# Attention with memories and a relu² MLP in one program: instructions left in the order of the kernel's own list schedule

## The chip, the cores and the metric

The kernel runs on one core of a Trainium2 chip. The metric is the device time of one execution in microseconds (us). A core has a matrix engine (PE in the profile), a vector engine (DVE), a scalar engine (ACT), a general engine (POOL), and a queue that starts transfers (SP). Each engine runs its own instructions one after the other and waits on semaphores for the others.

## The reference

Eight batches of eight heads, 576 tokens, head width 64, 32 memories. Attention reads from memories that are themselves sums over the tokens, and a two-layer MLP follows.

```python
a = softmax(phi, axis=2)                      # (8, 8, 576, 32), over the tokens' 32 weights
k_m = einsum('bhsm,bhsd->bhmd', a, k)         # 32 memories per head
v_m = einsum('bhsm,bhsd->bhmd', a, v)
attn = softmax(q @ k_m^T / 8) @ v_m           # (8, 8, 576, 64)
x = attn.transpose(0, 2, 1, 3).reshape(4608, 512)
out = relu(x @ w_in) ** 2 @ w_out             # w_in 512 x 2048, w_out 2048 x 512, given as 64-bit floats
```

## The kernel before

**What is computed in which form.** Products are wanted to the accuracy of 32-bit floats, so that each operand of the large products is split in a high and a low part (fp32r), and three products are summed: high by high, high by low, low by high. The kernel does not form x. For each batch it keeps the attention weights (ath high, atl low: 256 rows, as 8 heads of 32 memories, by 576 tokens), and for each slice of 256 of the 2048 hidden columns the product of the memories' values with w_in, called vw. The hidden product is then h = vw by at (L740), with a contraction of 256 instead of 512.

**Weights.** They come as 64-bit floats and are read as pairs of 32-bit words into a tile "raw" (L322). `decode` (L310 to L364) makes a high and a low part of them with some five DVE instructions (L324 to L357), ACT casts and, for some blocks, three PE matmuls into a tile pd. The parts of w_in are also written back to memory (L364, by POOL's queue), from which `wi_again` (L369, by SP's queue) reloads them for later pairs of batches. w_out's parts stay on the chip as 16 tiles wo. All decoding lies in the first 200 us or so.

**Order of the work.** Batches 0 and 1 go first, mixed with the decoding (n=0). Then come pairs of batches n=1, 2, 3 (batches 2 and 3, 4 and 5, 6 and 7). For a pair: `memory` makes the memories of its heads from phi, k and v; `attention` the weights at; then, for each slice s of 8, `vw_step` (L525 to L547) makes vw for both batches of the pair in two halves hh=0, 1, and two `step`s of the first batch use it. A step g is one block of 128 hidden columns of one batch (128 steps in all; batch 4 has steps 64 to 79). The second batch's 16 steps follow with the same vw.

**A vw half.** Six matmuls (L536) sum into one PSUM tile pvw (tag pv, one bank for all of them). Then, for each half of 64 partitions and each of two column ranges, ACT casts a piece of the tile into the high part of vw (L260, 64 by 256) and DVE subtracts that from the tile to get the low part (L545): four casts and four subtractions before the bank is free for the next pvw.

**A step.** `mm1` multiplies the two token ranges (0 to 256 is h_0, 256 to 576 is h_1; two PSUM banks for h), with six matmuls each (L740). A relu into r follows on ACT (L744) or DVE (L745), whichever the planner chose; then on ACT the square gh of the first 512 tokens, rounded to fp32r (L746), and gl of the last 64 (L747); the exact square r² of all 576 (L748 on ACT, or L749 on DVE); and on DVE the low parts glo (L750) and gl (L751). `mm2` adds to four accumulators acc: for each a matmul with gh and wo's high part (L770) and one with its low part (L771), then one with glo (L773). `mm2_left` (L796) does the last 64 tokens of both batches. At a batch's end the accumulators are copied and stored.

**What sets the order.** None of the functions issues anything at once. Each records operations with `plan.op`: the engines that may do it with an assumed duration, what it reads and writes, and a closure. `Plan.order` (L99 to about L184) is a list schedule: from assumed durations and latencies it works out a due time for each operation, then hands each engine, at each moment, the ready operation that is due first. In this schedule an operation can start once those before it in its data and its buffers have ended, and casts and subtractions of one pvw tile may overlap. The result is sorted by planned start time, and the last loop (L905) calls the closures in this order, which emits the instructions. The framework under it (`tile.TileContext`) tracks tiles, sets the semaphores, and has a scheduler of its own, which in the kernel before may still place the emitted instructions of each engine in another order.

Of the kernel before, what the change touches and what calls it, by code (L numbers as in the profile page):

```python
# [206 lines left out]
def tile_attention_moe(  # L207
# [41 lines left out]
    plan = Plan()  # L249
# [652 lines left out]
        for ff in range(NFF):  # L902
            step(pos[b1, ff])

    for o in plan.order():  # L905
        o.fn(o.left)


# [28 lines left out]
```

## Time and profile before

| what | value |
|---|---|
| median of 3 runs (their range) | 814.89 us (814.53 to 815.09) |
| the profiled execution, and its span | 814.6 us, all of it span |
| instructions | 13267 |
| PE busy | 776.2 us, 95% |
| DVE, ACT, POOL busy | 66%, 49%, 8% |
| read and written in memory | 79.17 MB, 17.83 MB |

A row of the timeline gives the start, the duration, the engine, the line, the operation, the tile written and those read with their shapes, how many instructions the row joins (x2), and in brackets the idle time of the engine before it with what ended it. Matmuls are pipelined, so that a row's duration is longer than the step from one matmul to the next. A row that joins instructions may enclose others that begin between its own. PEld is the loading of weights into PE, which goes on beside its matmuls.

### The profile page before, as it was taken

How to read it: one execution, taken by the hardware profiler on the slowest of the kernel's cores; microseconds unless marked ns; L12 is line 12 of the kernel's file. 1: busy time of each engine (PE TensorE's matmuls, PEld its weight loads, DVE VectorE, ACT ScalarE, POOL GpSimd, SP SyncE). 2: the span in 40 equal slices, each digit the busy share in tenths (PEclk: the TensorE clock that was granted, in tenths of full speed). 3: DMA queues.
4: the chain of work that ended last, by engine and by line, in shares of the span. 5: the costliest groups of instructions: out<-in, count | busy, mean ns of one | idle time of the engine just before them, and what ended most of it. 6: DMA issues, size and time to landing. Idle time of an engine off the chain costs nothing.

```text
span 814.6 us, 13267 instructions
## 1 busy us (share of the span) xinstructions
PE 776.2 (95%) x4926; PEld 652.5 (80%) x4926; DVE 536.4 (66%) x1190; ACT 403.1 (49%) x922; POOL 63.8 (8%) x103
## 2 busy tenths in 40 slices
PE   4889999999999999999999999999999999999995
PEld 2567888778887888888778888888788888888884
DVE  4678888783468976766776556877677556864540
ACT  2557766675653465634445355644334355643220
POOL 4012202320100100010000100010000100000000
PEclk9999999999999999999999999999999999999998
DMA  7969967666456523423443433513422433100001
GB/s 225 270 191 286 270 176 239 188 170 191 125 146 189 165 81 105 129 37 90 132 125 88 126 106 104 136 34 91 133 58 70 122 108 104 30 24 29 1 1 64
DMA packets 99716, 101.04 MB, mean 124 GB/s; under 512 B 32260, under 2 KB 85508, under 8 KB 99652
## 3 DMA queue, kind: packets, MB, share of 16 engines
q1 hardware_dynamic: 89188, 81.55, 34.2%
q0 software_dynamic: 10464, 18.65, 8.8%
q8 instruction: 39, 0.64, 0.3%
q14 instruction: 25, 0.20, 0.1%
HBM read 79.17 MB, written 17.83 MB: 119 GB/s over the span
## 4 chain that ended last, share of the span: by engine, by line
PE 73%; DVE 8%; issue 6%; DMA 5%; ACT 4%; SPq 1%; POOL 1%; DVEq 0%; POOLq 0%; ACTq 0%
PE h L740 20%; PE acc L770 12%; PE acc L773 12%; PE acc L771 12%; PE accl L796 5%; PE pvw L536 4%; PE psc L574 3%; PE pkv L426 2%; DMA raw<-in_moe_w_out_dram 1%; DMA phi<-in_phi_dram 1%; ACT vw L260 1%; DMA raw<-in_moe_w_in_dram 1%; DMA wo<-work 1%; DVE glo L750 1%; DVE work L327 1%
## 5 line engine op out<-in xcount | busy, mean ns | idle before, releaser
L740 PE MATMUL h<-ath,vw 128*128 128x320 f32 (+1 forms) x1024 | 211.6, 298 | 1.1 <-ACT r L744 0.6
L770 PE MATMUL acc<-wo,gh 128*128 128x512 f32 x512 | 207.0, 404 | 1.8 <-ACT gh L746 1.6
L771 PE MATMUL acc<-wo,gh 128*128 128x512 f32 x512 | 201.7, 394 | 0.0
L740 PEld LDWEIGHTS h<-ath,vw 128*128 128x128 f32 x1024 | 171.0, 189 | 17.2 <-ACT r L744 1.7
L773 PE MATMUL acc<-wo,glo 128*128 128x512 f32 x512 | 162.1, 405 | 1.7 <-DVE glo L750 1.5
L260 ACT CAST vw<-pvw 64x256 fp32r<-64x256 f32 (+1 forms) x224 | 85.7, 397 | 74.5 <-PE pvw L536 35.4
L545 DVE TENSOR_TENSOR vw<-pvw,vw 64x256 fp32r<-64x256 f32 x192 | 78.8, 420 | 64.8 <-ACT vw L260 62.9
L770 PEld LDWEIGHTS acc<-wo,gh 128*128 128x128 f32 x512 | 96.4, 188 | 23.4 <-ACT gh L746 3.7
L740 PE MATMUL h<-atl,vw 128*128 128x320 f32 (+1 forms) x512 | 109.9, 295 | 0.0
L771 PEld LDWEIGHTS acc<-wo,gh 128*128 128x128 f32 x512 | 96.4, 188 | 16.6
L773 PEld LDWEIGHTS acc<-wo,glo 128*128 128x128 f32 x512 | 89.5, 189 | 19.5 <-DVE glo L750 6.2
L746 ACT ACTIVATE gh<-r 128x512 fp32r<-128x512 f32 x128 | 80.8, 632 | 43.4 <-DVE r L745 37.6
L750 DVE TENSOR_TENSOR glo<-r,gh 128x512 fp32r<-128x512 f32 x128 | 87.5, 684 | 21.4 <-ACT r L748 19.7
L744 ACT ACTIVATE r<-h 128x256 f32<-128x256 f32 (+1 forms) x149 | 60.1, 406 | 56.8 <-PE h L740 53.5
L745 DVE TENSOR_SCALAR r<-h 128x320 f32<-128x320 f32 (+1 forms) x107 | 48.9, 459 | 58.4 <-PE h L740 57.9
L740 PEld LDWEIGHTS h<-atl,vw 128*128 128x128 f32 x512 | 82.5, 189 | 0.7 <-issue 0.2
L747 ACT ACTIVATE gl<-r 128x64 fp32r<-128x64 f32 x128 | 32.8, 256 | 68.5 <-DVE r L745 66.5
L748 ACT ACTIVATE r<-r 128x576 f32<-128x576 f32 x94 | 64.5, 686 | 2.2
L796 PE MATMUL accl<-wo,gl 128*128 128x512 f32 x192 | 52.3, 397 | 0.1
L796 PEld LDWEIGHTS accl<-wo,gl 128*128 128x128 f32 x192 | 35.0, 188 | 7.2 <-DVE o L260 0.5
L536 PE MATMUL pvw<-wi,VTh 128*128 128x256 f32 x192 | 37.3, 286 | 0.6 <-issue 0.3
L749 DVE TENSOR_TENSOR r<-r 128x576 f32<-128x576 f32 x34 | 25.7, 756 | 15.8 <-ACT gh L746 14.4
(137 smaller groups left out, 854.3 us busy)
## 6 DMA issues: line engine op xcount, KB each, us to landing
wi<-w_in_hi SPq DMA_DIRECT2D x56, 256.0 KB
wi<-w_in_lo SPq DMA_DIRECT2D x56, 256.0 KB
KV<-in_k_dram SPq DMA_DIRECT2D x32, 256.0 KB
KV<-in_v_dram SPq DMA_DIRECT2D x32, 256.0 KB
raw<-in_moe_w_in_dram SPq DMA_DIRECT2D x16, 512.0 KB
raw<-in_moe_w_out_dram SPq DMA_DIRECT2D x16, 512.0 KB
q<-in_q_dram SPq DMA_DIRECT2D x24, 288.0 KB
out_dram<-o POOLq DMA_DIRECT2D x20, 256.0 KB, 7.7
```

The lines of the kernel that those rows point to most:

```text
L260: nc.scalar.copy(o, i) if e == "ACT" else ENG[e].tensor_copy(o, i)
L536: nc.tensor.matmul(pw()[:, x * SL:(x + 1) * SL], l()[:, 2 * hh + x, :], w(r, x), start=(i == 0), stop=(i == 2))
L545: vec({"DVE": tt(SL)}, lambda e, V=V, pr=pr, src=src: nc.vector.tensor_sub(V()[pr, 1, hh, :], src(), V()[pr, 0, hh, :].bitcast(F32)), [pw, ...
L740: nc.tensor.matmul(p()[:, 0:n], V()[:, l, hh, c0:c0 + P], x()[:, hh, cs], start=(i == 0), stop=(i == 5))
L744: op({"ACT": act(n) - 30, **({} if b < 2 else {"DVE": tt(n)})}, lambda e, cs=cs, n=n, p=p: nc.scalar.activation(r()[:, cs], p()[:, 0:n], A ...
L746: op({"ACT": act(SM)}, lambda e: nc.scalar.activation(gh(), r()[:, 0:SM], AF.Square), [r], [gh])
L748: op({"ACT": act(S), **({} if b < 2 else {"DVE": tt(S)})}, lambda e: nc.scalar.activation(r(), r(), AF.Square) if e == "ACT" else nc.vecto ...
L750: vec({"DVE": tt(SM)}, lambda e: nc.vector.tensor_sub(glo(), r()[:, 0:SM], gh().bitcast(F32)), [r, gh], [glo])
L770: nc.tensor.matmul(a(), gh()[:, c], t()[:, 0], start=f0, stop=False)
L771: nc.tensor.matmul(a(), gh()[:, c], t()[:, 1], start=False, stop=False)
L773: nc.tensor.matmul(a(), glo()[:, c], t()[:, 0], start=False, stop=f1)
L796: nc.tensor.matmul(a(), G()[:, l, :], t()[:, w], start=(ff == 0 and n == 0), stop=(ff == NFF - 1 and n == 2))
```

## The change

The last loop stands in a `with tc.manual_schedule()`. Inside it the framework places each engine's instructions as they are emitted, that is in the order of `plan.order()`. The operations, the engine of each, the tiles, the buffers and the dependencies between instructions stay as they are; semaphores still make an instruction wait for what it needs.

```diff
-    for o in plan.order():
-        o.fn(o.left)
+    with tc.manual_schedule():
+        for o in plan.order():
+            o.fn(o.left)
```

Three places follow, on three engines; numbers in names are those of batch or step, slice and half, and a running number at the end, which is higher by two after the change.

PE in the first batch of pair n=2, step 68 and slice 3: h68_0 is the first token range of the step, pvw2_3_1 the second half of slice 3. First before, then after.

```order
L740 MATMUL h68_1_5253<-ath4_4838,vw2_0_2_5113 128x320 x2
L740 MATMUL h68_0_5270<-ath4_4838,vw2_0_2_5113 128x256 x2
L740 MATMUL h68_0_5270<-atl4_4852,vw2_0_2_5113 128x256 x2
L740 MATMUL h68_0_5270<-ath4_4838,vw2_0_2_5113 128x256 x2
L536 MATMUL pvw2_3_1_5261<-wi2_3_1_5115,VTh21_4228 128x256 x2
L536 MATMUL pvw2_3_1_5261<-wi2_3_1_5115,VTl21_4233 128x256
L536 MATMUL pvw2_3_1_5261<-wi2_3_1_5115,VTh21_4228 128x256 x2
L536 MATMUL pvw2_3_1_5261<-wi2_3_1_5115,VTl21_4233 128x256
L773 MATMUL acc4_0_2_5061<-wo11_686,glo67_5220 128x512
```

The same place of PE after the change.

```order
L740 MATMUL h68_1_5255<-ath4_4840,vw2_0_2_5115 128x320 x2
L536 MATMUL pvw2_3_1_5263<-wi2_3_1_5117,VTh21_4230 128x256 x2
L536 MATMUL pvw2_3_1_5263<-wi2_3_1_5117,VTl21_4235 128x256
L536 MATMUL pvw2_3_1_5263<-wi2_3_1_5117,VTh21_4230 128x256 x2
L536 MATMUL pvw2_3_1_5263<-wi2_3_1_5117,VTl21_4235 128x256
L740 MATMUL h68_0_5272<-ath4_4840,vw2_0_2_5115 128x256 x2
L740 MATMUL h68_0_5272<-atl4_4854,vw2_0_2_5115 128x256 x2
L740 MATMUL h68_0_5272<-ath4_4840,vw2_0_2_5115 128x256 x2
L773 MATMUL acc4_0_2_5063<-wo11_688,glo67_5222 128x512
```

The pvw product and h68_0 have changed places. The same exchange stands in slices 3 to 6 of n=2 and of n=3, at eight places. In slice 2 of both, two matmuls of a pvw that stood ahead of L773 stand behind it.

ACT at the same step, before: the relu, gl and gh of step 68 and the casts from pvw2_3_1 into the two batches' vw.

```order
L744 ACTIVATE r68_5268<-h68_0_5270 128x256
L747 ACTIVATE gl68_5309<-r68_5268 128x64
L746 ACTIVATE gh68_5297<-r68_5268 128x512
L260 CAST vw2_0_3_5235<-pvw2_3_1_5261 64x256 x2
L748 ACTIVATE r68_5268<-r68_5268 128x576
L260 CAST vw2_1_3_5241<-pvw2_3_1_5261 64x256
L747 ACTIVATE gl69_5325<-r69_5307 128x64
L260 CAST vw2_1_3_5241<-pvw2_3_1_5261 64x256
L746 ACTIVATE gh69_5319<-r69_5307 128x512
```

ACT at the same step, after.

```order
L260 CAST vw2_0_3_5237<-pvw2_3_1_5263 64x256 x2
L260 CAST vw2_1_3_5243<-pvw2_3_1_5263 64x256
L744 ACTIVATE r68_5270<-h68_0_5272 128x256
L260 CAST vw2_1_3_5243<-pvw2_3_1_5263 64x256
L746 ACTIVATE gh68_5299<-r68_5270 128x512
L747 ACTIVATE gl68_5311<-r68_5270 128x64
L748 ACTIVATE r68_5270<-r68_5270 128x576
L746 ACTIVATE gh69_5321<-r69_5309 128x512
```

Three casts have moved ahead of the relu and the fourth ahead of gh68, and gl68 behind gh68. In n=1 the same kind of move puts gl and a cast ahead of r².

DVE near the start, before: the last mx of batch 1's memories, the first glo, and the decoding (work_524) of the block of w_in in raw_410.

```order
L409 TENSOR_REDUCE mx1_1_511<-phi1_1_322 128x128
L750 TENSOR_TENSOR glo0_583<-r0_521,gh0_550 128x512
L751 TENSOR_TENSOR gl0_553<-r0_521,gl0_553 128x64
L451 TENSOR_SCALAR rs1_0_593<-pkv1_0_526 128x1
L452 RECIPROCAL rs1_0_593<-rs1_0_593 128x1
L459 SCALAR_TENSOR_TENSOR kvx1_0_610<-pkv1_0_526,rs1_0_593,par_76 128x128 x2
L324 TENSOR_SCALAR work_524<-raw_410 128x512
L326 TENSOR_SCALAR work_524<-raw_410 128x512
```

DVE at the same place, after.

```order
L409 TENSOR_REDUCE mx1_1_513<-phi1_1_324 128x128
L324 TENSOR_SCALAR work_526<-raw_412 128x512
L326 TENSOR_SCALAR work_526<-raw_412 128x512
L327 SCALAR_TENSOR_TENSOR work_526<-work_526 128x512
L328 TENSOR_SCALAR work_526<-work_526 128x512
L340 SCALAR_TENSOR_TENSOR wi0_1_1_582<-raw_412,work_526 128x512
L750 TENSOR_TENSOR glo0_585<-r0_523,gh0_552 128x512
L751 TENSOR_TENSOR gl0_555<-r0_523,gl0_555 128x64
```

The decoding of the block has moved ahead of glo0 and of batch 1's memory. In the first 200 us some half of DVE's and ACT's instructions stand at other places among their neighbours, on PE about a tenth in the whole program, nearly all of them before 93 us. On SP loads of raw weights and reloads of w_in change places up to the start of n=1, and after it one load of k in each of batches 3 to 7.

## The prediction

> **What bounds the kernel now.** I read the page first, for the engine that carries the span.
>
> ```profile
> span 814.6 us, 13267 instructions
> PE 776.2 (95%) x4926; PEld 652.5 (80%) x4926; DVE 536.4 (66%) x1190; ACT 403.1 (49%) x922; POOL 63.8 (8%) x103
> ```
>
> PE (TensorE) is busy for 776.2 of 814.6 us, no other engine for more than 66%. A change of order removes no work, so it can only move the 38 us in which PE idles. The second view, busy time by stretch, says where those are (columns: stretch, length, busy us and instructions of each engine, granted clock, DMA share, GB/s).
>
> ```profile
> core 0: us, PE busy (x) PEld busy (x) DVE busy (x) ACT busy (x) POOL busy (x), PEclk, DMA share, GB/s
> 0.00:100.00 100.00, 81.51 (x702) 60.00 (x703) 70.61 (x159) 57.34 (x120) 23.58 (x39) 0.98 0.85 246
> 100.00:200.00 100.00, 93.26 (x550) 81.00 (x549) 74.72 (x152) 67.26 (x144) 19.24 (x25) 1.00 0.69 198
> 450.00:520.00 70.00, 69.75 (x391) 60.38 (x390) 42.11 (x96) 34.99 (x89) 3.11 (x5) 1.00 0.39 112
> 640.00:710.00 70.00, 69.75 (x393) 60.42 (x392) 43.61 (x100) 37.38 (x94) 1.33 (x2) 1.00 0.29 87
> ```
>
> PE lacks 18.49 us in the first 100 us and 6.74 in the second 100: 25.23 us, the ceiling of what a better order can win there. In the stages 450 to 520 and 640 to 710 it lacks 0.25 us of 70. There nothing can be won and every new wait is paid in full. These two are the stages in which the next pairs of batches (n=2, n=3) turn their weights into vw, and the order of instructions shows PE, ACT (ScalarE) and DVE (VectorE) changed exactly there. The third view is therefore the timeline of one such period, engine by engine.
>
> **The change, part A: the first wait, for the pvw bank.** All pvw products share one PSUM bank (tag pv), which four ACT casts (L260) and four DVE subtractions (L545) empty. Before, PE does the second half of the hidden product (h68_0, L740) and then the second pvw of the slice; the change puts pvw first. PE around such a place:
>
> ```profile
> 484.37 0.28 PE L536 MATMUL pvw<-wi,VTl 128*128 128x256 f32 x1
> 486.92 0.69 PE L740 MATMUL h<-ath,vw 128*128 128x320 f32 x4
> 487.45 0.40 PE L740 MATMUL h<-atl,vw 128*128 128x256 f32 x2
> 487.93 0.47 PE L536 MATMUL pvw<-wi,VTh 128*128 128x256 f32 x2
> ```
>
> ACT and DVE in the same time (in brackets the idle time before, and what ended it):
>
> ```profile
> 484.68 0.64 ACT L260 CAST vw<-pvw 64x256 fp32r<-64x256 f32 x2 [1.60 <-PE pvw L536]
> 485.80 0.37 ACT L260 CAST vw<-pvw 64x256 fp32r<-64x256 f32 x1 [0.48 <-DVE vw L545]
> 486.65 0.37 ACT L260 CAST vw<-pvw 64x256 fp32r<-64x256 f32 x1 [0.48 <-DVE vw L545]
> ```
> ```profile
> 485.35 0.42 DVE L545 TENSOR_TENSOR vw<-pvw,vw 64x256 fp32r<-64x256 f32 x1 [1.42 <-ACT vw L260]
> 486.20 0.42 DVE L545 TENSOR_TENSOR vw<-pvw,vw 64x256 fp32r<-64x256 f32 x1 [0.43 <-ACT vw L260]
> 487.05 0.77 DVE L545 TENSOR_TENSOR vw<-pvw,vw 64x256 fp32r<-64x256 f32 x2 [0.43 <-ACT vw L260]
> ```
>
> The two engines never read the bank at the same time: cast, cast, subtraction, cast, subtraction, cast, two subtractions, each waiting for the one before. From pvw's end (484.65) to the last subtraction (487.82) this takes 3.17 us. The planner lets casts and subtractions overlap and so expects the bank earlier. PE reaches the new place of pvw when h68_1's last pair of matmuls is issued, one pair's 0.24 us before 487.45: at 487.21. It then stands until the bank is free. Taking 487.93 for that, as now, the wait is 0.72 us.
>
> [...]
>
> **Part A: the second wait, for gh68.** The second change at these places is on ACT: before, relu (L744), gl, gh (L746) and only then the casts of the second pvw; after, the casts are laid around the relu, and gh stands behind the fourth. A period now:
>
> ```profile
> 476.95 0.40 PE L740 MATMUL h<-atl,vw 128*128 128x256 f32 x2
> 477.43 0.47 PE L536 MATMUL pvw<-wi,VTh 128*128 128x256 f32 x2
> 478.10 0.28 PE L536 MATMUL pvw<-wi,VTl 128*128 128x256 f32 x1
> 480.28 0.40 PE L770 MATMUL acc<-wo,gh 128*128 128x512 f32 x1
> 481.89 0.39 PE L771 MATMUL acc<-wo,gh 128*128 128x512 f32 x1
> 482.28 1.20 PE L773 MATMUL acc<-wo,glo 128*128 128x512 f32 x4
> ```
> ```profile
> 477.62 0.39 ACT L744 ACTIVATE r<-h 128x256 f32<-128x256 f32 x1 [1.09 <-PE h L740]
> 478.05 0.62 ACT L746 ACTIVATE gh<-r 128x512 fp32r<-128x512 f32 x1
> 479.33 0.69 ACT L748 ACTIVATE r<-r 128x576 f32<-128x576 f32 x1
> 481.33 0.37 ACT L260 CAST vw<-pvw 64x256 fp32r<-64x256 f32 x1 [0.77 <-DVE vw L545]
> ```
> ```profile
> 481.55 0.67 DVE L750 TENSOR_TENSOR glo<-r,gh 128x512 fp32r<-128x512 f32 x1
> ```
>
> One such period is 10.50 us (pvw at 477.43 and again at 487.93). Let S be the start of the second pvw in the new order. It ends at S+0.95 (477.43 to 478.38). By the durations above: casts one and two to S+1.65, subtraction to S+2.08, cast three to S+2.48, relu to S+2.84 beside two subtractions that end at S+3.37, cast four to S+3.77, gh68 (0.62) to S+4.42. PE itself, with the same matmuls as now between 476.71 (0.24 before 476.95) and 480.28, reaches the first product with gh68 (L770) at S+3.57. Starting at about S+4.45 it waits 0.88 us. Back from this goes 0.15: before L773 PE now stands from 482.13 (481.89 and one step of 0.24) to 482.28 for glo, and in the new order r² and glo are done at S+6.07, while PE has its eight products only at S+6.30.
>
> Together 0.72 + 0.88 - 0.15 = 1.45 us a period. The exchange stands in slices 3 to 6 of n=2 and of n=3, 8 places: **+11.6 us**. Bounds: only the first wait bites and the 0.15 goes, 8 x 0.57 = 4.6; at the other end both, with nothing given back, 8 x 1.60 = 12.8. I take 11.6, since the rows fix each step of the chain; a shift of a few tenths moves one wait into the other rather than away.
>
> **Part B: slice 2 of both stages.**
>
> ```profile
> 471.39 0.42 PE L536 MATMUL pvw<-wi,VTh 128*128 128x256 f32 x2
> 472.02 1.20 PE L773 MATMUL acc<-wo,glo 128*128 128x512 f32 x4 [0.20 <-DVE glo L750]
> ```
>
> Before, two matmuls of a pvw fill PE's wait for glo; after, they stand behind L773. What filled the gap becomes idle: 0.42 us by its row, and up to 0.63, the whole stretch from 471.39 to 472.02. I take 0.54, between the two, twice: **+1.1 us** (0 to 1.3).
>
> **Part C: n=1, about 280 to 340 us.** After, ACT does gl and a third cast before r² (L748).
>
> ```profile
> 299.63 0.69 ACT L748 ACTIVATE r<-r 128x576 f32<-128x576 f32 x1
> 300.38 0.67 DVE L750 TENSOR_TENSOR glo<-r,gh 128x512 fp32r<-128x512 f32 x1
> 302.29 1.09 PE L773 MATMUL acc<-wo,glo 128*128 128x512 f32 x4
> ```
>
> With gl (0.26) and the cast (0.37, behind a subtraction) in front, r² ends at 301.15 instead of 300.32; on DVE two subtractions and a relu then go ahead of glo, which is ready at 302.43, against PE's 302.29. That is 0.15 us in six periods: **+0.9 us** (0 to 2).
>
> **Part D: the first 200 us.** Here the weights are decoded on DVE, and half of all its instructions move.
>
> ```profile
> 47.55 1.27 DVE L409 TENSOR_REDUCE mx<-phi 128x128 f32<-128x640 f32 x1
> 51.75 0.69 DVE L750 TENSOR_TENSOR glo<-r,gh 128x512 fp32r<-128x512 f32 x1 [2.93 <-ACT r L748]
> 53.59 0.41 DVE L324 TENSOR_SCALAR work<-raw 128x512 f32<-128x512 f32 x1
> ```
> ```profile
> 41.08 0.49 SPq L322 DMA_DIRECT2D raw<-in_moe_w_in_dram  x1
> ```
>
> DVE stands 2.93 us for r of the first step, with a block of weights that was asked for at 41.08 lying undecoded until 53.59. After, that block's five DVE instructions stand ahead of glo and can fill the hole. Against that, DVE now waits in order: an instruction whose block is late holds all behind it, glo among them. And PE's need here is set by loads as well (the DMA share is 0.85). The gain has the hole, 2.93 us, and as much again from the other stretch of idle PE as its edge (-5, rounded in); the loss is one such hole put in front of glo (+3). No row fixes the value; I take half a hole, **-1.5 us**.
>
> On SP, decode blocks and reloads of weights change places up to the start of n=1, and after that one load of K in each of batches 3 to 7 moves four places back; on POOL the write-outs of decoded weights change places among themselves. In n=2 and n=3 no load of weights for pvw moves, so I cost the queues at nothing there: the DMA share of 0.29 to 0.39 is the cover. A load that came late all the same would show as a wait before L536. What the queues do in the first 200 us lies within part D's bounds.
>
> Sum: 11.6 + 1.1 + 0.9 - 1.5 = +12.1 us on the profiled execution's 814.6, which lies 0.3 us under the median of the runs, 814.89. Forecast: 814.89 + 12.1 = **827.0 us**.
>
> **The rivals.**
> - *Faster.* The list order was meant for these engines, and the other order hides its loss where PE idles. For it: 25.23 us of idle PE, and the 2.93 us hole. Against it: the two stages with 0.25 us of slack. It needs the waits of part A to vanish, by casts that come earlier than I walk them, B with them, and part D at its edge of -5, with C's 0.9: 814.9 - 5 + 0.9 = 810.8. Chance 0.10.
> - *Half the price.* The periods re-phase, so that only one of the two waits bites: 4.6 + 1.1 + 0.9 - 3 = +3.6, about 818.5. Chance 0.12.
> - *The bank is shared by halves.* Casts and subtractions of different halves overlap: four casts back to back (0.64 a pair, 1.3) and a last subtraction (0.42), 1.7 to 2.1 us, less than the 2.56 from 484.65 to 487.21. Then both waits of part A vanish and B's lasts: 1.1 + 0.9 - 1.5, 815.4. [...] The waits for one another in the rows speak against it, and the change adds no freedom there. Chance 0.04.
> - *No effect,* because the engines' orders come out alike: the order of the changed program excludes it, PE, ACT and DVE differ at the places named. Left is that gains and losses cancel. Chance 0.03.
> - *Slower than forecast.* In-order waits for loads in the first 200 us cost more than a hole: 12.8 + 1.3 + 2 + 3 and a second hole of 3 make +22, so 837. Chance 0.10.
>
> **How the numbers follow.** The forecast itself has 0.61: 827, with 820 to 833 from its terms' bounds. The range goes from 815 (which takes in half price and the shared bank) to 834; outside lie the faster rival and most of the slowest one. A measurement of this kernel can tell some 0.2%, 1.6 us, from no change, so "same" is 813.3 to 816.5. Faster 0.11; same 0.07 (shared bank, cancellation); slower 0.82.
>
> **What would show it.** In the changed trace's stages n=2 and n=3 the period must grow from 10.50 to about 11.95 us; PE idle of 0.7 us before L536, released by DVE vw L545, and of 0.9 before L770, released by ACT gh L746, 8 times each. The idle of PE by stretch should be 6 us higher in each of the two stages, and within a few us of 25 in the first 200. Periods of 10.50 would prove part A wrong; a total change made before 200 us would prove part D wrong, whatever the sum.

## The result and the profile after

The changed kernel takes 827.82 us (median; 827.10 to 829.45) against 814.99 us of the kernel before (four runs, 814.53 to 821.47). The ratio on record is 1.0126, with a 95% interval of 1.0076 to 1.0175; the two medians alone give 1.0157. The forecast was 827.0 in a range of 815 to 834. The profiled executions differ by 11.6 us in span.

The page of the changed kernel, span and busy time:

```profile
span 826.2 us, 13317 instructions
PE 779.5 (94%) x4926; PEld 654.9 (79%) x4926; DVE 538.9 (65%) x1190; ACT 395.6 (48%) x922; POOL 64.5 (8%) x103
```

The count of work instructions is the same on every engine. PE's busy time differs by 3.3 us, so at least the other 8.3 of the 11.6 us are PE standing still. Busy time by stretch says where (columns as in the prediction):

```profile
0.00:100.00 100.00, 82.69 (x710) 63.09 (x711) 72.72 (x162) 58.71 (x123) 24.30 (x39) 0.95 0.84 245
100.00:200.00 100.00, 97.60 (x581) 86.20 (x580) 73.19 (x150) 69.66 (x151) 19.16 (x24) 1.00 0.68 199
280.00:340.00 60.00, 58.96 (x334) 51.05 (x333) 41.11 (x93) 33.04 (x86) 0.00 (x0) 1.00 0.33 99
450.00:520.00 70.00, 63.95 (x348) 54.09 (x347) 37.47 (x86) 31.71 (x81) 2.70 (x4) 1.00 0.34 99
640.00:710.00 70.00, 64.33 (x352) 54.74 (x351) 36.57 (x85) 30.90 (x79) 2.69 (x4) 1.00 0.32 95
```

Two things happened, with opposite signs. In the two stages of n=2 and n=3, PE's idle time rose from 0.25 us to 6.05 and 5.67 in 70 us. Between 100 and 200 us it fell from 6.74 to 2.40 us.

The waits of PE over the whole changed program (total, times, longest) name the two waits that part A of the prediction walked:

```profile
PE acc L770 <- ACT gh L746: 9.0, 13, 1.4
PE pvw L536 <- PE h L740: 4.4, 8, 0.6
```

Eight waits before pvw, and thirteen before the first product with gh: eight at the places of part A, three ahead of these (two in n=2, one in n=3), two in the first 200 us. One place of n=2 in PE's timeline, both waits of it (480.23 to 481.31 belongs to the period before):

```profile
480.23 0.40 PE L740 MATMUL h<-ath,vw 128*128 128x256 f32 x2
481.31 0.50 PE L770 MATMUL acc<-wo,gh 128*128 128x512 f32 x1 [0.68 <-ACT gh L746]
487.76 0.46 PE L740 MATMUL h<-ath,vw 128*128 128x320 f32 x2
488.76 0.48 PE L536 MATMUL pvw<-wi,VTh 128*128 128x256 f32 x2 [0.55 <-PE h L740]
```

and DVE's and ACT's rows that release them:

```profile
487.89 0.77 DVE L545 TENSOR_TENSOR vw<-pvw,vw 64x256 fp32r<-64x256 f32 x2 [0.43 <-ACT vw L260]
```
```profile
491.25 0.38 ACT L744 ACTIVATE r<-h 128x256 f32<-128x256 f32 x1
492.27 0.37 ACT L260 CAST vw<-pvw 64x256 fp32r<-64x256 f32 x1 [0.64 <-DVE vw L545]
492.67 0.63 ACT L746 ACTIVATE gh<-r 128x512 fp32r<-128x512 f32 x1
```

The pair of matmuls at 487.76 hands over after 0.29 us, at 488.05; pvw starts at 488.76, 0.71 us later (forecast 0.72). The row's own figure is 0.55, because the modelled end of the last matmul covers the beginning of a wait. It names PE's h as the releaser, which had long been done: what ended just before is the last subtraction, at 488.66. In the same way PE could go on at 480.47 and starts L770 at 481.31, 0.84 us later (forecast 0.88). And the ACT rows show why: the relu is done at 491.63, and gh, which needs it, starts at 492.67, behind the fourth cast, which itself waits for a subtraction.

The period has grown as forecast. The second pvw of slices 3, 4 and 5 of n=2 in the changed kernel:

```profile
476.74 0.96 PE pvw L536 x6
488.76 0.96 PE pvw L536 x6
500.80 0.96 PE pvw L536 x6
```

That is 12.02 and 12.04 us from one to the next, against 10.50 before (477.43 to 487.93) and 11.95 in the forecast.

**The lead, step by step.** A single time mixes the two signs, so from here on the kernels are compared step by step. Each step g has four L771 matmuls; the start of the first in one trace less that in the trace of before is the kernel's lag at that step (negative: a lead). Step 68 of before, for example, starts its first L771 at 480.51; the changed kernel at 481.65.

| kernel | step 1 | 19 | 31 | 43 | 63 | 66 | 74 | 95 | 98 | 106 | 127 |
|---|---|---|---|---|---|---|---|---|---|---|---|
| the change | 2.96 | -10.28 | -6.25 | -2.45 | -2.27 | -0.17 | 5.63 | 5.07 | 5.78 | 11.81 | 11.52 |
| first200 | 0.35 | -12.88 | -9.06 | -8.52 | -9.12 | -9.12 | -9.12 | -9.03 | -9.06 | -9.08 | -9.03 |
| rest200 | 1.68 | -1.27 | -0.70 | 3.24 | 3.07 | 5.19 | 11.03 | 10.63 | 11.30 | 17.30 | 17.02 |
| gh_first | 6.33 | -6.98 | -3.65 | 0.69 | 0.94 | 3.05 | 6.70 | 7.38 | 8.11 | 11.94 | 12.57 |
| h0_first | 3.61 | -9.66 | -6.08 | -1.57 | -1.34 | 0.79 | 6.58 | 5.99 | 6.65 | 12.59 | 12.38 |
| both_back | 3.79 | -9.48 | -5.90 | -1.44 | -1.69 | 0.42 | 1.01 | 0.85 | 1.58 | 2.24 | 2.20 |
| r2_first | 0.14 | -13.11 | -9.08 | -2.63 | -1.97 | 0.18 | 6.02 | 5.76 | 6.47 | 12.43 | 12.21 |
| glo_first | 3.98 | -9.28 | -4.74 | -1.85 | -1.94 | 0.20 | 6.04 | 5.54 | 6.24 | 12.22 | 12.01 |
| lat | 7.19 | -6.08 | -2.41 | 3.56 | 3.33 | 4.34 | 7.82 | 6.96 | 6.49 | 10.17 | 10.04 |
| first200_dve | 11.19 | -1.23 | 1.95 | 1.87 | 1.74 | 1.74 | 1.77 | 1.17 | 1.11 | 1.07 | 1.09 |
| first200_notdve | 7.17 | -5.99 | -1.23 | -1.38 | -0.88 | -0.88 | -0.87 | -1.35 | -1.41 | -1.41 | -1.36 |
| first150 | 1.95 | -9.13 | -8.80 | -8.91 | -9.28 | -9.28 | -9.30 | -9.52 | -9.58 | -9.61 | -9.60 |

In the kernel before, steps 1, 19 and 31 begin at 58, 189 and 255 us. Steps 0 to 31 are n=0 with the decoding, 32 to 63 n=1, 64 to 95 n=2, 96 to 127 n=3. The eight places of part A lie between steps 66 and 74 and between 98 and 106. The change loses 5.80 and 6.03 us there: 11.83, or 1.48 a place. Two things limit the table. All lags are taken against one trace of before. And equal steps are not quite equal work: ahead of step 1 PE has issued 395 matmuls in the kernel before and 412 in the list's order, while at step 31 both have issued 1679, so that the lag at step 31 compares like with like, and the one at step 1 does not.

### The profile page after: what moved, and what is told of

It is laid out like the page before. It is cut to its first block, busy times and chain, and to the rows that moved or that the text cites. A ratio compares the mean times of both kernels' runs of the same rounds, so it can differ in the third digit from the quotient of the medians.

```text
span 826.2 us, 13317 instructions
## 1 busy us (share of the span) xinstructions
PE 779.5 (94%) x4926; PEld 654.9 (79%) x4926; DVE 538.9 (65%) x1190; ACT 395.6 (48%) x922; POOL 64.5 (8%) x103
## 5 line engine op out<-in xcount | busy, mean ns | idle before, releaser
L770 PE MATMUL acc<-wo,gh 128*128 128x512 f32 x512 | 208.1, 406 | 9.0 <-ACT gh L746 9.0
L740 PE MATMUL h<-ath,vw 128*128 128x320 f32 (+1 forms) x1024 | 211.6, 297 | 0.7 <-DVE r L745 0.3
L771 PE MATMUL acc<-wo,gh 128*128 128x512 f32 x512 | 201.4, 393 | 0.0
L740 PEld LDWEIGHTS h<-ath,vw 128*128 128x128 f32 x1024 | 170.7, 188 | 17.3 <-ACT r L744 3.1
L773 PE MATMUL acc<-wo,glo 128*128 128x512 f32 x512 | 161.4, 404 | 1.0 <-DVE glo L750 0.7
L770 PEld LDWEIGHTS acc<-wo,gh 128*128 128x128 f32 x512 | 96.3, 188 | 32.5 <-ACT gh L746 12.4
L771 PEld LDWEIGHTS acc<-wo,gh 128*128 128x128 f32 x512 | 96.3, 188 | 16.7
L740 PE MATMUL h<-atl,vw 128*128 128x320 f32 (+1 forms) x512 | 109.5, 295 | 0.0
L773 PEld LDWEIGHTS acc<-wo,glo 128*128 128x128 f32 x512 | 90.1, 189 | 17.3 <-DVE glo L750 3.1
L745 DVE TENSOR_SCALAR r<-h 128x320 f32<-128x320 f32 (+1 forms) x107 | 48.8, 462 | 63.9 <-PE h L740 62.9
L740 PEld LDWEIGHTS h<-atl,vw 128*128 128x128 f32 x512 | 82.1, 188 | 0.3 <-DVE atl L675 0.3
L536 PEld LDWEIGHTS pvw<-wi,VTh 128*128 128x128 f32 x192 | 31.3, 188 | 12.6 <-PE h L740 6.3
L828 POOL DMA_DIRECT2D out_dram<-o x20 | 13.1, 660 | 277.3 <-DVE o L260 143.1
```

Of the source, the lines that this page charges most:

```text
L536: nc.tensor.matmul(pw()[:, x * SL:(x + 1) * SL], l()[:, 2 * hh + x, :], w(r, x), start=(i == 0), stop=(i == 2))
L740: nc.tensor.matmul(p()[:, 0:n], V()[:, l, hh, c0:c0 + P], x()[:, hh, cs], start=(i == 0), stop=(i == 5))
L770: nc.tensor.matmul(a(), gh()[:, c], t()[:, 0], start=f0, stop=False)
L771: nc.tensor.matmul(a(), gh()[:, c], t()[:, 1], start=False, stop=False)
L773: nc.tensor.matmul(a(), glo()[:, c], t()[:, 0], start=False, stop=f1)
```

## The experiments

All times of before stand beside those of the kernels that ran with it; its own runs spread from 809.65 to 821.56 us over the four sets, for a reason that stays open, so that 2 to 3 us of a difference between kernels' times can be told only by step.

### Where the gain and the loss are: the list order early alone, and late alone

```diff
+    order = plan.order()
+    cut = sum(o.start < 200000 for o in order)
     with tc.manual_schedule():
-        for o in plan.order():
+        for o in order[:cut]:
             o.fn(o.left)
+    for o in order[cut:]:
+        o.fn(o.left)
```

> Emission order is kept only for operations that the planner starts before its own 200 us; the rest is left to the framework as in the kernel before. By step, the changed kernel led the kernel before by 10.3 us at its step 19 (199.62 us) and by 6.3 at step 31. Theory (the early order is a gain that the late order spends): 804.6 to 808.6 us, 806 the likeliest, 6 to 10 less than before. Rival (the lead is borrowed, because decoding is put off and must be made up): 812 to 815, the lead of step 19 gone by step 31.

Measured: 807.84 us against 814.92, ratio 0.9894 (0.9855 to 0.9933). The other half has the first loop outside and the second inside `manual_schedule`.

> The other way round: the framework orders what the planner starts before 200 us, and emission order is kept from there on. Theory: the losses of the changed kernel after step 31 (3.9 us in n=1, 7.5 and 6.3 in n=2 and n=3) come without the early gain: 832 to 835 us. Rival (the late losses come from the early lead itself, as work that runs ahead and then waits): about 815 to 820.

Measured: 832.99 us against 814.92, ratio 1.0204 (1.0164 to 1.0243). Both theories hold. (The step 19 of the first expectation begins at 189.06 us in the kernel before and at 178.78 in the changed one; its 199.62 is neither.) From step 31 to the end the change loses 17.77 us, the late half alone 17.72, and the early half alone 0.03. So the late loss has nothing to do with the early lead, and the early lead is not borrowed: first200 still has 9.03 of its 12.88 us at the end. Its median is also the lowest of all kernels here, below both that were compared.

What goes away early is seen in PE's waits between 100 and 200 us. The kernel before (total, times, longest):

```profile
PE pvw L516 <- ACT vw L260: 2.0, 2, 1.6
PE acc L770 <- ACT gh L746: 1.6, 2, 0.9
PE patl L671 <- DVE atl L668: 1.5, 1, 1.5
PE acc L773 <- DVE glo L750: 1.3, 1, 1.3
```

The early half alone, its stretch and its longest wait:

```profile
100.00:200.00 100.00, 98.13 (x583) 86.08 (x581) 71.40 (x146) 70.19 (x152) 19.15 (x24) 1.00 0.67 198
```
```profile
PE pkv L442 <- DVE asum L432: 0.8, 1, 0.8
```

The waits for casts, gh, atl and glo (1.3 to 2.0 us each) are gone or down to 0.3, and PE's idle time there falls from 6.74 to 1.87 us. That decoding stood ahead of these results on ACT and DVE is read from the order; it was not tested by itself.

### Which engine's order makes the early gain

The same early region, with `engines=` the set {DVE}, and with the set of all others.

> As the run that kept emission order for the first 200 us alone (807.84 us), but on DVE only; all other engines are ordered by the framework. Theory (the early gain comes from decoding put ahead of glo and the memories on DVE): 806 to 809. Rival (it comes from PE's and ACT's order, with DVE following): 813 to 816.

Measured: 816.58 us against 815.68, ratio 0.9991 (0.9962 to 1.0021).

> The complement: emission order in the first 200 us on PE, ACT, POOL and SP, with DVE ordered by the framework. Theory (DVE's order makes the gain): 812 to 816. Rival (PE's and ACT's): 806 to 809. If both kernels land near 811, the gain needs the orders together.

Measured: 814.50 us against 815.68, ratio 0.9984 (0.9957 to 1.0011). Neither half of the engines makes the gain in time, so neither theory holds for both kernels. By step it is stranger: from step 1 to step 31 both lead by as much as the full early order (9.24 and 8.40, against 9.41 us), but they reach step 1 at +11.19 and +7.17 us, against +0.35. Mixed orders lose before 58 us what they win after it. A part of that goes with the clock: its mean in 20 to 60 us was 0.83 in both of these executions, against 0.96 with the full early order and in the kernel before. The executions of both_back and glo_first (below) have the list's order on all engines there, the same 0.83, and reach step 1 at +3.79 and +3.98 us. These two less the 0.35 us of the full early order are 3.44 and 3.63: by this estimate the clock makes some 3.5 us of either lag, and the mixed orders themselves some 7 and 3 us. Which instruction's order starts it stays open.

### Whether the early gain needs the cut at 200 us

The cut moved to 150 us.

> Emission order kept for what the planner starts before 150 us, the rest ordered by the framework. With the cut at 200 us the time was 807.84 us; there the lead was 13.0 us at step 19 and 9.8 at step 21. Theory (the late part of the decoding, between 150 and 200 us, gains nothing from the list order that lasts): 805 to 809. Rival (the lead is made by keeping decoding behind glo up to 200 us): 809 to 813.

Measured: 810.93 us against 816.32, ratio 0.9926 (0.9898 to 0.9955). By step the theory holds: from step 1 to step 31 this kernel gains 10.75 us, the one with the cut at 200 us 9.41, which gives 3.24 us back between steps 19 and 21; here nothing is given back. By time it is not shown to be better: its runs lie between 806.75 and 812.09 us, with a mean clock of 0.984 to 0.991, those of the other between 806.74 and 808.52, in another set and at 0.992 to 0.997.

### Part A: one wait at a time

In the first kernel, gh of the step is moved ahead of the fourth cast (ACT's order alone changes), in the second h_0 ahead of pvw (PE's order alone). `ahead(o, of)` moves operation o in the list ahead of the first one of `of`; `casts` and `subs` are those of one pvw in the list's order. The diff is shortened: each kernel has only its own line of the two.

```diff
+    order = plan.order()
+    for n in (2, 3):
+        for s in range(3, 7):
+            g = pos[2 * n, 2 * (s - 1)]
+            ahead(named["gh", g], casts[3:])                       # gh_first
+            ahead(named["h", g, 0], [named["pvw", n, s, 1]])       # h0_first
     with tc.manual_schedule():
-        for o in plan.order():
+        for o in order:
```

> The changed kernel, with gh of the step put ahead of the fourth cast on ACT at the eight places of part A; PE's order unchanged. Theory (two waits, the second because gh stands behind the fourth cast): the wait before L770 goes, 8 x 0.83 = 6.6 us less than the changed kernel, about 821; the wait before L536 stays. Rival (the second wait only follows from the first, because PE and the chain were late together): no change, 827 to 828.

Measured: 829.24 us against 814.92, ratio 1.0147 (1.0094 to 1.0201). The time says that nothing came back, but this execution was 3.37 us behind the changed kernel at step 1 already, before the edit. At the eight places it loses 3.65 + 3.83 = 7.48 us instead of 11.83, and 0.75 us right after the last place of each stage; over steps 63 to 127 it is 11.63 instead of 13.79. So 2.2 us come back, not 6.6. PE's waits over the program:

```profile
PE pvw L536 <- PE h L740: 4.4, 8, 0.6
PE acc L773 <- DVE glo L750: 3.4, 11, 0.6
PE acc L770 <- ACT gh L746: 3.4, 5, 1.4
```

The wait for gh is gone at the eight places (13 waits are 5), the one for the bank is untouched, and a new one stands before L773, for glo. DVE's rows of one place:

```profile
495.55 0.43 DVE L545 TENSOR_TENSOR vw<-pvw,vw 64x256 fp32r<-64x256 f32 x1 [0.48 <-ACT vw L260]
496.01 0.82 DVE L745 TENSOR_SCALAR r<-h 128x320 f32<-128x320 f32 x2
496.86 0.69 DVE L750 TENSOR_TENSOR glo<-r,gh 128x512 fp32r<-128x512 f32 x1
```

The fourth cast is now later by gh's 0.63 us, and with it the last subtraction, which in DVE's order stands ahead of two relus and glo. The wait was handed to the next in the row.

> The changed kernel, with h_0 put back ahead of pvw on PE at the eight places of part A; ACT's and DVE's order unchanged, so that casts of the pvw still stand ahead of the relu of h_0. Theory: the chain pvw, casts, subtractions, gh starts when the bank is free in both orders, so gh is ready at the same time and the wait before L536 only moves to L770: no change, 827 to 828.5. Rival (the two waits of 0.72 and 0.88 add up, each with its own cause): 8 x 0.72 = 5.8 us less, about 822.

Measured: 827.79 us against 814.92, ratio 1.0131 (1.0084 to 1.0179). The theory holds: 5.79 + 5.94 = 11.73 us are lost at the eight places, as with the change (11.83). PE's waits:

```profile
PE acc L770 <- ACT gh L746: 10.4, 13, 1.4
PE h L740 <- ACT r L744: 4.0, 7, 0.6
```

The bank's wait has vanished from the list, and gh's has grown from 9.0 to 10.4; a new one stands before L740, because the relu, which frees h, is still queued on ACT behind three casts. The theory named only the first of these.

### Part A: all three engines

At the eight places all three engines get back the order of before. The diff, again shortened, stands inside the same two loops; `behind` moves operations right behind another.

```diff
+            ahead(named["h", g, 0], [named["pvw", n, s, 1]])
+            for name in ("relu", "gl", "gh", "r2"):
+                key = (name, g, 0) if name == "relu" else (name, g)
+                ahead(named[key], casts[2:] if name == "r2" else casts)
+            behind(subs[1:3], named["relu", g + 1, 1])
+            behind(subs[3:], named["glo", g])
```

> The changed kernel, with the eight places of part A set back to what the kernel before has on all three engines: h_0 ahead of pvw on PE; relu, gl and gh ahead of the casts and r2 ahead of the third on ACT; the relu of the next step after the first subtraction and the last subtraction behind glo on DVE. Theory (the loss is one circle of order over three engines, which single moves on one engine can't undo): the periods go back to 10.5 us, 8 x 1.45 = 11.6 us less than the changed kernel, about 816. Rival (the loss is the planner's order elsewhere in these stages): no more than 3 us come back, as in the run with gh alone ahead.

Measured: 819.40 us against 816.32, ratio 1.0035 (1.0007 to 1.0063). At the eight places 0.59 + 0.66 = 1.25 us are left of 11.83. The stage of n=2, busy time and PE's waits:

```profile
450.00:520.00 70.00, 67.74 (x377) 57.98 (x376) 40.44 (x92) 33.30 (x86) 2.70 (x4) 1.00 0.37 107
```
```profile
PE acc L773 <- DVE glo L750: 1.2, 3, 0.4
PE acc L770 <- ACT gh L746: 1.1, 2, 0.7
```

The bank's waits are gone, and the two that stay of gh's stand ahead of the first place (at 452.83 and 469.87), where nothing was touched. So 10.58 of the 11.83 us belong to these few instructions, on the three engines together; over steps 63 to 127 this kernel loses 3.89 us instead of 13.79. The median is above the 816 us that the theory expected; the ten runs go from 815.17 us at a mean clock of 0.997 to 822.49 at 0.985.

### Part C: what holds glo in n=1

In steps 36, 38, 40 and 42, r2 moves ahead of the third cast on ACT; in the second kernel also, on DVE, the next step's relu and glo move ahead of the second subtraction (shortened).

```diff
+        ahead(named["r2", g], casts[2:])
+        ahead(named["relu", g + 1, 1], subs[1:])   # second kernel only
+        ahead(named["glo", g], subs[1:])           # second kernel only
```

> The changed kernel, with the exact square of steps 36, 38, 40 and 42 (slices 3 to 6 of n=1) put ahead of the third cast on ACT. Read by step from step 35 to step 43, where the changed kernel lost 1.9 us against before. Theory (the prediction's part C: glo is late because r2 ends late on ACT): 0.3 us of each of the four periods come back, 1.2 us. Rival (glo is late because DVE has three subtractions and a relu ahead of it, which wait for the third cast): nothing comes back, or the periods get longer by up to 0.4 us, since the third cast is now later.

Measured: one run, 828.77 us. From step 35 to 43 the change lost 1.91 us (-4.36 to -2.45), this kernel 4.06 (-6.69 to -2.63). DVE and PE at one of the four steps:

```profile
305.75 0.43 DVE L545 TENSOR_TENSOR vw<-pvw,vw 64x256 fp32r<-64x256 f32 x1 [0.98 <-ACT vw L260]
306.73 0.42 DVE L545 TENSOR_TENSOR vw<-pvw,vw 64x256 fp32r<-64x256 f32 x1
307.07 0.67 DVE L750 TENSOR_TENSOR glo<-r,gh 128x512 fp32r<-128x512 f32 x1
```
```profile
307.80 1.20 PE L773 MATMUL acc<-wo,glo 128*128 128x512 f32 x4 [0.70 <-DVE glo L750]
```

DVE idles 0.98 us for the third cast with glo behind it: the earlier r2 makes glo later. The rival holds.

> The same four steps of n=1 with r2 ahead of the third cast on ACT and, on DVE, the relu of the next step and glo ahead of the second subtraction, as the kernel before has it. Theory of part C and the rival with DVE's order both expect the 1.9 us between steps 35 and 43 to come back (1.4 to 2.0); together with the run before, it says which engine's order held glo. If the loss stays here too, it lies in PE's own order.

Measured: one run, 828.92 us; the loss from step 35 to 43 is 0.68 us (-2.53 to -1.85). The glo that is to be used at 310.28 now runs ahead of the last two subtractions:

```profile
308.70 0.69 DVE L750 TENSOR_TENSOR glo<-r,gh 128x512 fp32r<-128x512 f32 x1 [0.19 <-ACT r L748]
```
```profile
310.28 1.09 PE L773 MATMUL acc<-wo,glo 128*128 128x512 f32 x4
```

PE no longer waits for it; 1.2 of the 1.9 us came back, a little less than expected. What held glo in n=1 is DVE's order, and r2's place on ACT only helps when DVE's changes with it.

### The planner's price

```diff
-                    [pw, (V, (hh, 0, hf))], [(V, (hh, 1, hf))], port=None, lead=True)
+                    [pw, (V, (hh, 0, hf))], [(V, (hh, 1, hf))], port=None, lead=True, lat=1050 if hf and x else 120)
```

> The changed kernel with one number of the planner changed: the last subtraction of a pvw half has a latency of 1050 ns instead of 120, so that the planner holds the bank as long as the trace shows (3.17 us instead of about 2.25). Emission order is kept everywhere. Theory (the planner's wrong price of the bank is the root of parts A to C): the losses of n=2 and n=3 (13.8 us) at least halve and n=1 does not grow: 810 to 821. Rival (the list schedule is wrong at these places for other reasons, the shared ACT and DVE queues): 824 to 830.

Measured: 824.36 us against 816.32, ratio 1.0105 (1.0066 to 1.0144), in the rival's range. By step the theory is half right: over steps 63 to 127 the loss halves, from 13.79 to 6.71 us, but n=1 gets worse, from 3.80 to 5.97 us between steps 31 and 43. With the bank priced as the trace shows it, the list schedule finds other orders with other waits. PE's waits in n=2 with this planner:

```profile
PE acc L770 <- ACT gh L746: 2.3, 4, 0.6
```

The wait of gh behind the casts is still there at four places, since the new number prices the bank and not the casts that wait for subtractions in between.

## Why the prediction was right, and where it was not

- **What bounds the kernel.** Right: PE has no slack in the two stages (0.25 us of idle in 70 before), and the new waits were paid in full there. The idle time rose by 5.80 and 5.42 us, where 6 had been named as the sign; in the first 200 us 19.71 us are left, 5.5 less than the 25.23 of before.
- **Part A, +11.6 us.** Right in mechanism, and nearly in size: waits of 0.71 and 0.84 us against 0.72 and 0.88, and a period that grows by 1.52 to 1.57 us, against 1.45. The 11.83 us of the table begin with slice 2's step, where 1.35 us are won back (part B); without that step and up to the second step behind the last place (67 to 76, 99 to 108) the eight places lose 6.17 + 6.22 = 12.39 us. It was called two waits with a price each, and of these "only the first wait bites" was kept as the lower bound. The runs show one chain over three engines: taking either wait away on one engine gives back 0.1 or some 2 us, since the next instruction in the chain is late then. Changing all three gives back some 10.
- **Part B, +1.1 us.** The number is near, the mechanism is wrong. The step that failed is "What filled the gap becomes idle". In the changed kernel's slice 2 of n=2 there is no gap ahead of the first product with glo (L773), and likewise in n=3:

```profile
471.01 0.39 PE L771 MATMUL acc<-wo,gh 128*128 128x512 f32 x1
471.23 1.07 PE L773 MATMUL acc<-wo,glo 128*128 128x512 f32 x4
```

PE had stood for gh just before, and glo had ended at 470.81. In this step the lag even fell (-0.17 to -0.92 in n=2, 5.78 to 5.18 in n=3: 1.35 us). The losses lie at the entries of the two stages (steps 63 to 66 and 95 to 98), 2.10 + 0.71 = 2.81 us; together that is 1.46. In n=2, three waits stand there that the prediction did not price:

```profile
443.34 0.47 PE L536 MATMUL pvw<-wi,VTh 128*128 128x256 f32 x2 [0.53 <-DVE vw L545]
452.25 0.50 PE L770 MATMUL acc<-wo,gh 128*128 128x512 f32 x1 [0.38 <-ACT gh L746]
469.28 0.50 PE L770 MATMUL acc<-wo,gh 128*128 128x512 f32 x1 [0.68 <-ACT gh L746]
```

- **Part C, +0.9 us, bounds 0 to 2.** The step that failed is "0.15 us in six periods". n=1 lost 3.80 us from step 31 to 43, outside the bounds. Four periods lost 0.48 each on average and not 0.15, because three subtractions, and not two, stand ahead of glo; and 1.45 us went between steps 31 and 32, at the entry, where nothing was priced (0.44 us more lie between steps 32 and 35). DVE's rows at one of the four, behind a first subtraction at 295.62:

```profile
296.46 0.43 DVE L545 TENSOR_TENSOR vw<-pvw,vw 64x256 fp32r<-64x256 f32 x1 [0.43 <-ACT vw L260]
297.44 0.42 DVE L545 TENSOR_TENSOR vw<-pvw,vw 64x256 fp32r<-64x256 f32 x1
297.79 0.67 DVE L750 TENSOR_TENSOR glo<-r,gh 128x512 fp32r<-128x512 f32 x1
```

The cause given, a late r2 on ACT, was wrong: with r2 early the loss doubled.
- **Part D, -1.5 us, bounds -5 to +3.** The step that failed is "I take half a hole". The lead at step 31 was 6.25 us, beyond the edge; in first200, with the same early order and a mean clock in 20 to 60 us of 0.96 as in the kernel before, and not 0.87 as here, it was 9.06. The sum was made around one hole of DVE at 48.8 us. The lead comes from 82 to 189 us (steps 3 to 19), where it grows by 13.13 us; 4.03 of these are given back up to step 31. In that stretch PE's idle time falls from 6.74 to 0.34 us, as its waits for ACT and DVE go; in the prediction this idle time stood only as a ceiling. Another 4.41 us are work at another place and no gain by themselves: PE issues 572 matmuls there instead of 600, since between steps 3 and 4 28 are missing that the list's order does earlier. The prediction did not look at this.
- **The sum.** The forecast of +12.1 us is near the +11.6 of the traces by luck, because errors cancel: D was 4.8 us better than forecast, A, B and C together 4.1 us worse (12.39 + 1.46 + 3.80 against 13.6). The direction rests on part A, which alone outweighs D.
- **The range and the noise.** The bounds of the four terms add up to 814.5 to 834, the whole range; the 820 to 833 that the prediction calls "its terms' bounds" do not come out of them. And a measurement does not tell 0.2%: runs of the kernel before spread over 1.5%, and the interval of the ratio is 1% wide.
- **The rivals.** The faster one needed part A to vanish, and it did not. The bank shared by halves did not come: the rows of the changed kernel show casts and subtractions taking turns as before (at the place shown above two subtractions end at 490.95 and 492.24, and the casts after them start at 490.99 and 492.27). Re-phasing did not come either.

## What to carry to other kernels

A list schedule that is right in one part of a program and wrong in another can be kept for the one part: here the order by the planner's list wins some 9 us while weights are decoded and loses 17.8 us in the steady stages, and keeping it for the first 200 us alone gives a ratio of 0.9894. Where a wait passes through the queues of three engines, walk all three before moving an instruction in one; here moves on one engine gave back 0.1 and 2.2 us over steps 63 to 127, since the wait went to the next in the chain, and moves on all three 9.9 us. And where a change has parts of both signs, compare two traces at the same step, not two times.

## What the runs showed of the hardware

**The granted clock near the start differs from one execution to the next.** The kernels gh_first and r2_first have the same instructions in the same order up to 200 us. Busy time by stretch (the clock is the third number from the end), first of gh_first, then of r2_first:

```profile
28.12:31.53 3.41, 1.13 (x8) 0.80 (x8) 2.71 (x9) 2.51 (x6) 0.00 (x0) 1.00 1.07 369
31.53:45.19 13.66, 12.31 (x45) 8.70 (x44) 10.61 (x22) 6.26 (x12) 0.00 (x0) 0.50 1.02 249
```
```profile
31.53:45.19 13.66, 11.22 (x60) 7.14 (x60) 13.64 (x28) 8.15 (x17) 0.73 (x1) 1.00 1.02 251
```

gh_first ran at half clock for 13.66 us, and again from 52.01 to 55.43; r2_first did so nowhere before its end. The rows of the same matmuls are nearly twice as long at half clock, first in gh_first, then in r2_first:

```profile
39.84 2.08 PE L350 MATMUL pd<-work,ident 128*128 128x512 f32 x2 [0.68 <-ACT vw L260]
40.93 1.42 PE L351 MATMUL pd<-wo,minus 128*128 128x512 f32 x1
```
```profile
35.94 1.12 PE L350 MATMUL pd<-work,ident 128*128 128x512 f32 x2 [0.68 <-ACT vw L260]
36.50 0.80 PE L351 MATMUL pd<-wo,minus 128*128 128x512 f32 x1
```

Matmul by matmul, gh_first is 0.90 us behind r2_first just before its clock falls (30.93 against 30.03), 6.09 us at the end of the stretch (45.49 against 39.40), and 6.20 us behind the second one. At step 1 the two are 6.33 and 0.14 us behind the kernel before; from step 1 to step 31 they then gained 9.98 and 9.22. The six executions with this early order (r2_first, the change, h0_first, both_back, glo_first, gh_first) line up: mean clocks in 20 to 60 us of 1.00, 0.87, 0.87, 0.83, 0.83 and 0.79 go with lags at step 1 of 0.14, 2.96, 3.61, 3.79, 3.98 and 6.33 us. So most of the 6.2 us arises while the clock is halved. That is read from traces, since nothing here sets the clock. It does not explain the spread of the kernel before: beside the experiments its runs have mean clocks of 0.992 to 0.997, and those of 809.65 and of 820.10 us both 0.997.

What makes the clock fall, and why in one execution and not in the next, is not shown here. In the 3.41 us ahead of this fall PE's rows are busy for 1.13 us, and the clock stayed at half while they were busy for 12.31 of 13.66 us.

**Short waits on PE do not show in the idle time.** In the rows of the changed kernel the matmul before a wait has a modelled end some 0.16 us beyond the step to the next (0.40 against 0.24 us for a pair of 256 columns). So 0.71 us of standing shows as 0.55 and 0.84 as 0.68, and a wait under 0.16 us, by this estimate, not at all. In n=1 PE's waits list only 0.8 us between 280 and 345 us, while the kernel lost 2.35 us from step 32 to 43 there (-4.80 to -2.45); the starts of the steps showed it.
